# A fused dynamic-convolution and MLP kernel: its fill in another order, with small transposes as warm-up

## The chip, the cores and the metric

One core of a Trainium2 chip runs the whole program. The metric is the device time of one execution in microseconds (us); the time of a kernel is the median of its timed runs. The views of the profile come from one further execution, and durations are taken from that one.

## The reference

Three layers stand behind each other, in fp32. A dynamic convolution weighs the last seven rows of `x` with a softmax over `weight_gen` (2 x 4096 rows of 192, eight heads). A gated layer follows, with 1536 hidden columns, and a layer with `h * cos(h)`, with 2048.

```python
w = exp(weight_gen - max(weight_gen)); w = w / (sum(w) + 1e-9)
x = einsum('bshk,bskhg->bshg', w, x_unf)          # x_unf: seven shifted rows of x
x = (1 / (1 + exp(-(x @ w_gate))) * (x @ w_val)) @ w_out
h = x @ w_in
out = (h * cos(h)) @ w_out2
```

## The kernel before

The 8192 rows are worked on in 16 chunks of 512. A chunk's first layer has 12 steps, its second 8; a step computes two tiles of hidden columns (`hidden`, L413: 18 matmuls of 64 partitions, two row halves side by side), puts them through the nonlinearity, splits the result into a high and a low part (`gh` by ScalarE, `gl` by GpSimd, L556 and L557) and multiplies by the output weights (`out_matmuls`, L432). Every product is made of three: high by high, low by high, high by low.

The program is written in one fixed order (`tc.manual_schedule()`): each engine works off its instructions in the order in which the code issues them, and a wait holds up all that stands behind it on that engine.

The **fill** is what comes before the first full step:

- The softmax weights `sm` of the first two groups (`load_group`, L222; group 0 serves chunk 0, group 1 the next three quarters) and the first input `xp` (`load_x`, L266) are loaded, then the weight units (`Unit.load`, L137: each has a gate part and a value part; `OutUnit.load`, L169). Before the change, `sm` and the value parts of units 0 to 2 go over ScalarE's queue, the rest over SyncE's (SP).
- `softmax_ops` issues on VectorE the maximum (L237), the difference (L240), on ScalarE the exponential (L242), on VectorE sum (L245), reciprocal (L247, L248) and scaling (L251). `s0` and `s1` are the two groups.
- `conv_products(0)` issues the seven products of `xp` with the weights on VectorE (L283: four into `prs`, two into `pr`, one into `acc`). `first_input` transposes each of them on TensorE (`transposes`, L335: 16 matmuls of 64 columns a product, accumulated in the PSUM tiles `po0` and `po2`). Then `split_input` writes the transposed input `xT`: five high pieces each by ScalarE (L357) and VectorE (L359, a cast), then ten low pieces by VectorE (L363).
- A weight unit is decoded by `decode` in two parts: two ScalarE operations (L110, L113), then one of VectorE (L115). Afterwards `split` makes its high part on ScalarE (L120) and its low part on GpSimd (L122). `next(decoding)` issues one piece of that, `run(late)` the splits that have become due. 128x384 is one of the small units 0 and 1, 128x768 a large one or an output unit.
- `steps[:2]` then issue their 24 first matmuls (`mm_high`, L413), and the loop over the steps begins. The first step's product on VectorE is L518.

TensorE has nothing to do until the first product is ready. `warm_up(8)` gives it eight full 128x128 fp32 matmuls on the identity into the four rotating tiles `h`, which nobody reads.

Of the kernel before, what the change touches and what calls it, by code (L numbers as in the profile page):

```python
# [9 lines left out]
F32 = mybir.dt.float32  # L10
# [3 lines left out]
AF = mybir.ActivationFunctionType  # L14
# [15 lines left out]
def dyn_conv_glu_cos_mlp(  # L30
# [11 lines left out]
    nc = tc.nc  # L42
    B, S, D = x.shape
    H, K = weight_gen.shape[2], weight_gen.shape[3]
    G = D // H
    P = 128
# [4 lines left out]
    N = TC * P  # L51
# [6 lines left out]
    HP = P // 2  # L58
# [22 lines left out]
    ps_h = ctx.enter_context(tc.tile_pool(name="ps_h", bufs=4, space=bass.MemoryType.PSUM))  # L81
    ps_o = ctx.enter_context(tc.tile_pool(name="ps_o", bufs=1, space=bass.MemoryType.PSUM))

    ident = const.tile([P, P], F32, name="ident")
    sin_bias = const.tile([P, 1], F32, name="sin_bias")
    warm = const.tile([P, 1], F32, name="warm")
# [128 lines left out]
    def load_group(g, tag, q=nc.sync):  # L215
        t0, t1 = groups[g]
        pool = fpool if tag == "wf" else opool
        s = pool.tile([P, (t1 - t0) * H, K], F32, name="sm", tag=tag)
        cuts = sorted({t0, t1, min(max(t0, T - ROT), t1)})
        for a, b in zip(cuts, cuts[1:]):  # L220
            r = (a + ROT) % T
            q.dma_start(  # L222
                out=s[:, (a - t0) * H:(b - t0) * H, :].rearrange("p a k -> p (a k)"),
                in_=wgr[:, r:r + b - a, :].rearrange("p t c -> p (t c)"),
            )
        for t in range(t0, t1):
            sm[t] = (s, t0)
# [62 lines left out]
    def product_tile():  # L290
        return apool.tile([P, TC, D], F32, name="pr", tag="pr", bufs=2)
# [20 lines left out]
    def conv_products(c):  # L312

        big = tpool.tile([P, K - 3, TC, D], F32, name="prs", tag="xA" if c == LEAD else "xB")
        att[c] = [big[:, k] for k in range(K - 3)] + [product_tile(), product_tile(), acc_tile()]
        for k, pr in enumerate(att[c]):
            tap(c, k, pr)
            yield
# [10 lines left out]
    def transposes(p, src, first, end):  # L329

        blocks = [(0, 0)] + [(2, t) for t in range(TC)] + [(0, t) for t in range(1, TC)]
        for q, t in blocks:
            for h in range(2):
                r = slice(h * HP, (h + 1) * HP)
                nc.tensor.matmul(  # L335
                    p[h][0:min(P, D - q * HP), (2 * q + t) * HP:(2 * q + t + 1) * HP],
                    lhsT=src[r, t, q * HP:min(D, q * HP + P)], rhs=ident[r, r], is_transpose=True,
                    start=first and (q, t) == blocks[0], stop=end and (q, t) == blocks[-1],
                )

    WHOLE, HALVES = slice(0, P), (slice(0, HP), slice(HP, P))
# [49 lines left out]
    def first_input():  # L391

        p = [ps_o.tile([P, N], F32, name="pt", tag=f"po{2 * h}") for h in range(2)]
        for k, _ in enumerate(conv_products(0)):
            transposes(p, att[0][k], k == 0, k == K - 1)
            yield
        xt = xT[1, 0] = tpool.tile([P, 2, NQ, N], F32R, name="xT", tag="xA")
        ops = split_input(xt, p, True)
        next(ops)
        yield  # L400
        for _ in ops:
            pass
# [80 lines left out]
    class Step:  # L483
# [5 lines left out]
        ps = None  # L489
# [88 lines left out]

    TAPS = [1, 1, 2, 2, 0, 2, 1, 1, 1, 2, 1], [0, 0, 0, 2, 0, 2, 2, 2, 2, 2, 2]
    APART = 0, 1, 6, 7, 8, 10, 10  # L580
    NWARM = 8
    SOFT, TAPS0, AHEAD = [0,1,2,3,4], [4,5,6,7,8,9,9], 2
    LEAD = 2
    segments = [(1, c) for c in range(LEAD)]
# [44 lines left out]

    def warm_up(n):  # L630
        for _ in range(n):
            ps = ps_h.tile([P, N], F32, name="pw", tag="h")
            nc.tensor.matmul(ps[:, 0:P], lhsT=ident, rhs=ident, start=True, stop=True)

    def run(ops):
        for f in ops:
            f()
        ops.clear()

    with tc.manual_schedule():  # L640
        nc.gpsimd.memset(sin_bias, SIN_BIAS)
        make_identity(nc, ident)
        load_group(0, "va", nc.scalar)
        load_x(0)
        load_group(1, "o", nc.scalar)
        sp, act = nc.sync, nc.scalar
        units1[0].load(sp, 0)
        units1[0].load(act, 1)
        nc.scalar.activation(out=warm, in_=sin_bias, func=AF.Exp)
        units1[1].load(sp, 0)  # L650
        units1[1].load(act, 1)
        units1[2].load(sp, 0)
# [12 lines left out]
        decoding = chain(units1[:2] + [u for _, u in todo])  # L665
# [4 lines left out]
        s0, s1 = softmax_ops(0), softmax_ops(1)  # L670
        for c in range(1, NCH):
# [15 lines left out]
            if c <= LEAD:  # L687
                n, ops = K, conv_products(c)
# [4 lines left out]
            else:  # L693
                n, ops = 2 * K, conv_ops(c)
# [1 line left out]
            add_side(k0, at, [cost(TC * D)] * n, ops)  # L696
        side.sort(key=lambda e: e[1])

        for ops in [s0] * 3 + [s1] * 2 + [s0] * 2 + [s1] * 3:
            next(ops)  # L700
        nc.scalar.activation(out=warm, in_=sin_bias, func=AF.Sigmoid)
        units1[3].load(sp, 1)
        load_x(1)
        units1[4].load(sp, 0)
# [1 line left out]
        outs1[1].load(sp)  # L706
        for _ in s0:
            pass
        warm_up(NWARM)
        for k, _ in enumerate(first_input()):  # L710
            if k in (5, 6):
                next(decoding)
            if k == 5:
                run(late)
            if k == K:
                run(late)
                next(decoding)
                run(late)
# [24 lines left out]
        for k, st in enumerate(steps):  # L743
            layer, c, j = st.layer, st.c, st.j
            ended = None
            if layer == 1:
# [17 lines left out]
                if k in inputs:  # L764
                    c1 = inputs[k]
                    ops = transpose_ops(att[c1], c1)
# [76 lines left out]
```

## Time and profile before

| | us |
|---|---|
| median of 3 timed runs | 1252.81 (1251.09 to 1253.61) |
| profiled execution, its own time | 1251.61 |
| span of the profiled execution | 1249.8 |
| TensorE matmul busy | 1219.4 (98%) |
| VectorE busy | 902.1 (72%) |
| ScalarE busy | 792.8 (63%) |
| GpSimd busy | 713.0 (57%) |

PE is TensorE's matmuls and PEld its weight loads, which lie beside them; DVE is VectorE, ACT ScalarE, POOL GpSimd, and SPq and ACTq are the queues on which SyncE and ScalarE issue transfers. A row of the timeline merges instructions of one line that follow each other: start, time from the first start to the last end, engine, line, operation, count, and in brackets the idle time ahead of it with what ended that. A busy engine is not one that bounds: what matters is who waits for whom in a stretch.

### The profile page before, as it was taken

The numbers are of one execution on the slowest core, as the hardware profiler recorded it, in microseconds if no ns is written. First come the engines' busy times: TensorE is split into PE (matmuls) and PEld (weight loads), VectorE is DVE, ScalarE is ACT, GpSimd is POOL, SyncE is SP. The second block draws the span as 40 slices with busy tenths as digits, with TensorE's granted clock in tenths as the row PEclk, the third lists the DMA queues.
The fourth block names the chain that finished last, engine by engine and source line by source line (L and its number), as shares of the span: only waits on it lengthen the run. The fifth ranks groups of instructions, "written<-read, shape, count | busy, mean of one in ns | idle before, by whom it ended". The sixth has DMA issues, their size and how long they took to land.

```text
span 1249.8 us, 26898 instructions
## 1 busy us (share of the span) xinstructions
PE 1219.4 (98%) x11056; PEld 1058.3 (85%) x11056; DVE 902.1 (72%) x1309; ACT 792.8 (63%) x1326; POOL 713.0 (57%) x531
## 2 busy tenths in 40 slices
PE   6889999999999999999999999999999999999997
PEld 5677988898898888888898888989889899888886
DVE  7967887777877676877667787775877767683585
ACT  6765856648475574857557485664847557484674
POOL 3958645647465474655637465463746546464563
PEclk8999999999999999999999999999999999999999
DMA  9902202121111211111121120112111121020010
GB/s 250 248 20 58 63 14 69 27 70 27 45 32 34 69 26 54 43 45 27 26 82 27 46 52 14 58 27 74 27 45 26 40 58 26 14 52 14 1 27 26
DMA packets 27403, 61.94 MB, mean 50 GB/s; under 512 B 2580, under 2 KB 7698, under 8 KB 27280
## 3 DMA queue, kind: packets, MB, share of 16 engines
q1 hardware_dynamic: 26368, 59.09, 17.5%
q8 instruction: 86, 1.41, 0.5%
q10 hardware_dynamic: 912, 1.13, 0.3%
q14 instruction: 37, 0.30, 0.1%
HBM read 30.33 MB, written 6.29 MB: 29 GB/s over the span
## 4 chain that ended last, share of the span: by engine, by line
PE 84%; DVE 1%; ACT 1%; issue 0%; DVEq 0%; ACTq 0%
PE ph L413 46%; PE po L432 36%; PE pf L469 1%; PE pt L335 1%; DVE wk L546 0%; ACT wk L542 0%; ACT gh L556 0%; DVE wk L529 0%; DVE wk L532 0%; DVE wk L518 0%; ACT va L441 0%; DVE wk L537 0%; DVE gl L557 0%; ACT wk L536 0%; DVE pr L283 0%
## 5 line engine op out<-in xcount | busy, mean ns | idle before, releaser
L557 POOL TENSOR_TENSOR gl<-wk,gh 128x512 fp32r<-128x512 f32 x446 | 607.0, 1367 | 498.5 <-ACT gh L556 381.3
L413 PE MATMUL ph<-xT,unit 64*128 64x512 f32 x5760 | 772.8, 390 | 8.5 <-DVE wk L518 4.6
L413 PEld LDWEIGHTS ph<-xT,unit 64*128 64x128 f32 x5760 | 617.9, 185 | 104.0 <-DVE wk L518 13.6
L432 PE MATMUL po<-gh,outu 64*128 64x512 f32 x2688 | 552.1, 390 | 2.2 <-ACT gh L556 1.8
L432 PE MATMUL po<-gl,outu 64*128 64x512 f32 x1792 | 467.7, 389 | 4.6 <-POOL gl L557 4.6
L556 ACT ACTIVATE gh<-wk 128x512 fp32r<-128x512 f32 (+1 forms) x450 | 283.1, 629 | 249.1 <-DVE wk L518 206.1
L432 PEld LDWEIGHTS po<-gh,outu 64*128 64x128 f32 x2688 | 405.5, 185 | 37.2 <-ACT gh L556 2.7
L432 PEld LDWEIGHTS po<-gl,outu 64*128 64x128 f32 x1792 | 315.7, 185 | 28.8 <-POOL gl L557 6.4
L518 DVE TENSOR_TENSOR wk<-ph,wk 128x512 f32<-128x512 f32 x192 | 131.7, 686 | 146.4 <-ACT wk L515 136.0
L546 DVE SCALAR_TENSOR_TENSOR wk<-ph,wk 128x512 f32<-128x512 f32 (+1 forms) x258 | 168.4, 687 | 42.5 <-ACT wk L542 42.5
L542 ACT ACTIVATE wk<-wk,sin_bias 128x512 f32<-128x512 f32 (+1 forms) x258 | 173.0, 714 | 19.4 <-DVE wk L532 8.8
L515 ACT ACTIVATE wk<-ph 128x512 f32<-128x512 f32 x192 | 113.6, 592 | 57.8 <-PE ph L413 56.9
L529 DVE TENSOR_SCALAR wk<-ph 128x512 f32<-128x512 f32 x129 | 88.0, 682 | 64.1 <-PE ph L413 62.3
L536 ACT ACTIVATE wk<-ph 128x512 int32<-128x512 f32 x129 | 75.5, 585 | 73.6 <-PE ph L413 73.0
L309 DVE TENSOR_TENSOR acc<-acc,pr 128x768 f32<-128x768 f32 x78 | 102.0, 1308 | 0.4
L283 DVE TENSOR_TENSOR pr<-xp,sm 128x768 f32<-128x768 f32 x84 | 96.0, 1144 | 0.0
L532 DVE SCALAR_TENSOR_TENSOR wk<-wk,ph 128x512 f32<-128x512 f32 x129 | 88.1, 683 | 4.4
L537 DVE TENSOR_TENSOR wk<-wk,ph 128x512 f32<-128x512 int32 x129 | 87.3, 677 | 0.0
L442 DVE TENSOR_TENSOR va<-po,va 128x512 f32<-128x512 f32 x32 | 22.0, 688 | 39.1 <-PE po L432 29.1
L363 DVE TENSOR_TENSOR xT<-pt,xT 64x256 fp32r<-64x256 f32 (+1 forms) x76 | 27.2, 413 | 21.5 <-ACT xT L357 21.3
L357 ACT ACTIVATE xT<-pt 64x256 fp32r<-64x256 f32 (+1 forms) x66 | 20.4, 378 | 21.5 <-PE pt L335 21.3
L122 POOL TENSOR_TENSOR unit<-wf,unit 128x768 fp32r<-128x768 f32 (+1 forms) x11 | 22.2, 2022 | 15.8 <-ACT unit L120 15.8
(61 smaller groups left out, 507.8 us busy)
## 6 DMA issues: line engine op xcount, KB each, us to landing
xT<-xT SPq DMA_DIRECT2D x90, 256.0 KB, 3.9
xp<-in_x_dram SPq DMA_DIRECT2D x13, 960.0 KB, 4.8
out_dram<-o SPq DMA_DIRECT2D x16, 384.0 KB, 2.3
rawo<-in_moe_w_out_dram SPq DMA_DIRECT2D x7, 768.0 KB, 15.9
raw<-in_moe_w_in_dram SPq DMA_DIRECT2D x8, 384.0 KB, 15.7
raw<-in_moe_w_gate_dram SPq DMA_DIRECT2D x5, 384.0 KB, 12.8
raw<-in_moe_w_val_dram SPq DMA_DIRECT2D x4, 384.0 KB, 15.3
sm<-in_weight_gen_dram SPq DMA_DIRECT2D x3, 336.0 KB, 5.1
```

Of the source, the lines that this page charges most:

```text
L283: nc.vector.tensor_tensor(out=out.rearrange("p t (h g) -> p t h g", g=G), in0=xp[c][:, k:k + TC, :].rearrange("p t (h g) -> p t h g", g=G) ...
L309: nc.vector.tensor_tensor(out=acc, in0=acc, in1=last, op=ALU.add)
L413: nc.tensor.matmul(ps[i], lhsT=u.t[r, w, (s + i) % NQ, c0:c0 + P], rhs=xt[r, x, s, :], start=n == 0, stop=n == len(terms) - 1,)
L432: nc.tensor.matmul(po[2 * i + a], lhsT=w[r, d0:d0 + P], rhs=g[r], start=first and g is gh and d0 < D, stop=last and g is gl,)
L515: nc.scalar.activation(out=self.w[0], in_=self.ps[0], func=AF.Sigmoid)
L518: nc.vector.tensor_tensor(out=self.w[0], in0=self.ps[1], in1=self.w[0], op=ALU.mult)
L529: nc.vector.tensor_scalar(out=w, in0=u, scalar1=0.25, scalar2=ROUND_MAGIC, op0=ALU.add, op1=ALU.add)
L532: nc.vector.scalar_tensor_tensor(out=w, in0=w, scalar=ROUND_MAGIC, in1=u, op0=ALU.subtract, op1=ALU.subtract)
L542: nc.scalar.activation(out=w, in_=w, func=AF.Sin, scale=-SIN_SCALE, bias=sin_bias)
L546: nc.vector.scalar_tensor_tensor(out=w, in0=self.ps[i][:, r], scalar=TWO_PI, in1=w, op0=ALU.mult, op1=ALU.mult)
L556: nc.scalar.activation(out=gh, in_=w, func=AF.Copy)
L557: eng.tensor_tensor(out=gl, in0=w, in1=gh.bitcast(F32), op=ALU.subtract)
```

## The change

- **Queues.** Both `sm` loads go over SP's queue, around the first input; ScalarE's queue starts with the table load and has the value parts alone.
- **Softmax.** The two differences of group 1 and its exponential move behind the second product; so does the load of the sigmoid table.
- **Decoding.** The decoding of unit 0 on VectorE moves behind the last product, that of unit 1 and the whole of unit 2 behind the high pieces of `xT`.
- **Warm-up.** Instead of eight large matmuls there are rounds of two small transposes (one in each row half): 24 rounds ahead of the first product, 4, 4, 4, 4, 4 and 2 behind the next six, 10 behind the last. They write the tiles `po1` and `po3`, of which there is one buffer each.

```diff
     def first_input():
         p = [ps_o.tile([P, N], F32, name="pt", tag=f"po{2 * h}") for h in range(2)]
+        warm_up(24)
         for k, _ in enumerate(conv_products(0)):
             transposes(p, att[0][k], k == 0, k == K - 1)
+            warm_up(WARM[k])
             yield
...
-    NWARM = 8
+    WARM = 4, 4, 4, 4, 4, 2, 10
...
     def warm_up(n):
         for _ in range(n):
-            ps = ps_h.tile([P, N], F32, name="pw", tag="h")
-            nc.tensor.matmul(ps[:, 0:P], lhsT=ident, rhs=ident, start=True, stop=True)
+            for r in HALVES:
+                ps = ps_o.tile([P, N], F32, name="pw", tag="po1" if r is HALVES[0] else "po3")
+                nc.tensor.matmul(ps[:, 0:HP], lhsT=ident[r, :], rhs=ident[r, r], is_transpose=True, start=True, stop=True)
...
-        load_group(0, "va", nc.scalar)
+        sp, act = nc.sync, nc.scalar
+        load_group(0, "va")
         load_x(0)
-        load_group(1, "o", nc.scalar)
-        sp, act = nc.sync, nc.scalar
+        load_group(1, "o")
+        nc.scalar.activation(out=warm, in_=sin_bias, func=AF.Exp)
         units1[0].load(sp, 0)
         units1[0].load(act, 1)
-        nc.scalar.activation(out=warm, in_=sin_bias, func=AF.Exp)
...
-        for ops in [s0] * 3 + [s1] * 2 + [s0] * 2 + [s1] * 3:
+        for ops in [s0] * 3 + [s1] * 2 + [s0] * 2:
             next(ops)
-        nc.scalar.activation(out=warm, in_=sin_bias, func=AF.Sigmoid)
...
-        warm_up(NWARM)
         for k, _ in enumerate(first_input()):
-            if k in (5, 6):
+            if k == 1:
+                for _ in range(3):
+                    next(s1)
+                nc.scalar.activation(out=warm, in_=sin_bias, func=AF.Sigmoid)
+            if k == K - 1:
                 next(decoding)
-            if k == 5:
                 run(late)
             if k == K:
+                next(decoding)
                 run(late)
                 next(decoding)
                 run(late)
```

On TensorE, at the start of the program, the order before was this (`pw` is a warm-up's tile, `pt` the transposed products):

```order
L633 MATMUL pw<-ident 128x128 x8
L335 MATMUL pt<-ident,prs 128x64 x2
L335 MATMUL pt<-ident,prs 64x64 x8
L335 MATMUL pt<-ident,prs 128x64 x8
L335 MATMUL pt<-ident,prs 64x64 x8
```

Now it is this, with the semaphore that an instruction waits for in brackets (PE_49 counts TensorE's own finished instructions, DVE_49 those of VectorE, Pool_49 those of GpSimd):

```order
L636 MATMUL pw<-ident 128x64 [waits Pool_49]
L636 MATMUL pw<-ident 128x64
L636 MATMUL pw<-ident 128x64 [waits PE_49] x46
L335 MATMUL pt<-ident,prs 128x64 [waits DVE_49]
L335 MATMUL pt<-ident,prs 128x64
L335 MATMUL pt<-ident,prs 64x64 x8
L335 MATMUL pt<-ident,prs 128x64 x6
L636 MATMUL pw<-ident 128x64 [waits PE_49] x8
```

Every warm-up but the first two waits for TensorE's own earlier one, since a half's tile has one buffer: it waits for the warm-up two places ahead of it.

On VectorE, from the last small products to the low pieces of the transposed input, the order before was this (`wf` is a unit being decoded, from `raw`):

```order
L283 TENSOR_TENSOR pr_165<-xp_103,sm_101 128x768
L115 SCALAR_TENSOR_TENSOR wf_269<-wf_269,raw_107 128x384
L283 TENSOR_TENSOR acc_166<-xp_103,sm_101 128x768
L115 SCALAR_TENSOR_TENSOR wf_273<-wf_273,raw_111 128x384
L359 CAST xT_300<-pt_162 128x4x64
L359 CAST xT_300<-pt_162 64x4x64 x4
L115 SCALAR_TENSOR_TENSOR wf_297<-wf_297,raw_114 128x768
L363 TENSOR_TENSOR xT_300<-pt_161,xT_300 128x4x64
```

Now it is this:

```order
L283 TENSOR_TENSOR pr_241<-xp_103,sm_101 128x768
L283 TENSOR_TENSOR acc_242<-xp_103,sm_101 128x768
L115 SCALAR_TENSOR_TENSOR wf_494<-wf_494,raw_108 128x384
L359 CAST xT_504<-pt_142 128x4x64
L359 CAST xT_504<-pt_142 64x4x64 x4
L115 SCALAR_TENSOR_TENSOR wf_498<-wf_498,raw_111 128x384
L115 SCALAR_TENSOR_TENSOR wf_516<-wf_516,raw_114 128x768
L363 TENSOR_TENSOR xT_504<-pt_141,xT_504 128x4x64
```

The last product stands one decoding earlier; the decoding of unit 1 has moved from ahead of the casts to behind them, ahead of the low pieces.

On ScalarE, around its high pieces of `xT` (L357), the order before was this:

```order
L120 ACTIVATE unit_276<-wf_269 128x384
L110 ACTIVATE wf_297<-raw_114 128x768
L113 ACTIVATE raw_114<-raw_114 128x768
L357 ACTIVATE xT_300<-pt_161 128x4x64
L357 ACTIVATE xT_300<-pt_161 64x4x64 x4
L120 ACTIVATE unit_311<-wf_273 128x384
```

Now it is this:

```order
L120 ACTIVATE unit_501<-wf_494 128x384
L357 ACTIVATE xT_504<-pt_141 128x4x64
L357 ACTIVATE xT_504<-pt_141 64x4x64 x4
L110 ACTIVATE wf_516<-raw_114 128x768
L113 ACTIVATE raw_114<-raw_114 128x768
L120 ACTIVATE unit_519<-wf_498 128x384
```

The two operations on unit 2 (`raw_114`) have moved behind the high pieces. Behind this place the engines' orders are the same in both kernels.

## Rows read from the trace of the kernel before

**Rows 1.** Busy time by stretch: us of each engine (instructions), PEclk, DMA share, GB/s.

```profile
24.00:62.00 38.00, 31.84 (x296) 23.91 (x297) 34.27 (x33) 29.77 (x45) 36.18 (x21) 1.00 1.04 248
...
100.00:600.00 500.00, 497.91 (x4542) 435.25 (x4540) 374.04 (x545) 320.05 (x538) 290.55 (x214) 1.00 0.16 44
```

**Rows 2.** Timeline of VectorE, 0 to 26 us.

```profile
6.21 0.39 DVE L237 TENSOR_REDUCE st<-sm 128x32 f32<-128x224 f32 x1 [6.21 <-DMA sm<-in_weight_gen_dram]
...
7.35 0.67 DVE L237 TENSOR_REDUCE st<-sm 128x32 f32<-128x224 f32 x2
...
8.82 0.62 DVE L240 TENSOR_TENSOR sm<-sm,st 128x224 f32<-128x224 f32 x2
...
9.78 3.57 DVE L283 TENSOR_TENSOR prs<-xp,sm 128x768 f32<-128x768 f32 x4
...
15.00 0.55 DVE L115 SCALAR_TENSOR_TENSOR wf<-wf,raw 128x384 uint32<-128x384 uint32 x1
15.47 0.95 DVE L283 TENSOR_TENSOR acc<-xp,sm 128x768 f32<-128x768 f32 x1
16.34 0.55 DVE L115 SCALAR_TENSOR_TENSOR wf<-wf,raw 128x384 uint32<-128x384 uint32 x1
17.24 2.23 DVE L359 CAST xT<-pt 128x256 fp32r<-128x256 f32 x5 [0.34 <-PE pt L335]
19.49 0.96 DVE L115 SCALAR_TENSOR_TENSOR wf<-wf,raw 128x768 uint32<-128x768 uint32 x1
20.37 3.86 DVE L363 TENSOR_TENSOR xT<-pt,xT 128x256 fp32r<-128x256 f32 x10
...
25.44 0.68 DVE L518 TENSOR_TENSOR wk<-ph,wk 128x512 f32<-128x512 f32 x1
```

**Rows 3.** Timeline of TensorE, 0 to 26 us, and its first 16 transposes alone.

```profile
1.40 3.59 PE L633 MATMUL pw<-ident 128*128 128x128 f32 x16 [1.40 <-POOL ident masks.py:199]
10.80 1.11 PE L335 MATMUL pt<-ident,prs 64*128 64x64 f32 x16 [5.81 <-DVE prs L283]
16.48 0.69 PE L335 MATMUL pt<-ident,acc 64*128 64x64 f32 x16 [0.65 <-DVE acc L283]
18.82 5.20 PE L413 MATMUL ph<-xT,unit 64*128 64x512 f32 x27 [0.21 <-ACT xT L357]
```

**Rows 4.** Waits from 24 to 62 us: who for whom, us in total, times, longest.

```profile
ACT gh L556 <- DVE wk L518: 6.3, 7, 1.5
```

**Rows 5.** Transfers: GB/s from 2 to 6 us, and two loads' KB and us to landing.

```profile
2.00:4.00 2.00, 2.00 (x11) 2.00 (x11) 0.00 (x0) 1.49 (x2) 0.00 (x0) 1.00 0.75 260
4.00:6.00 2.00, 0.99 (x6) 0.79 (x5) 0.00 (x0) 0.00 (x0) 0.00 (x0) 1.00 0.99 389
...
xp<-in_x_dram SPq DMA_DIRECT2D x1, 960.0 KB, 5.2
...
sm<-in_weight_gen_dram ACTq DMA_DIRECT2D x1, 224.0 KB, 6.0
```

**Rows 6.** Transposes by tile: ns of one, min/median/max, first and last start.

```profile
L335 PE MATMUL pt<-ident,prs x64: 311/312/367, 10.8 to 14.2; 64*128 64x64 f32 x32, 64*64 64x64 f32 x32
L335 PE MATMUL pt<-ident,acc x16: 216/220/273, 16.5 to 16.9; 64*128 64x64 f32 x8, 64*64 64x64 f32 x8
```

**Rows 7.** Busy time and PEclk (third number from the end) in stretches of 2 us.

```profile
10.00:12.00 2.00, 1.20 (x22) 1.21 (x24) 2.00 (x3) 1.98 (x5) 0.00 (x0) 0.50 1.07 220
...
14.00:16.00 2.00, 1.83 (x42) 1.64 (x38) 2.00 (x4) 0.41 (x1) 0.00 (x0) 0.78 1.10 274
...
18.00:20.00 2.00, 1.77 (x7) 1.15 (x9) 1.88 (x5) 1.92 (x5) 0.00 (x0) 0.58 1.06 288
```

**Rows 8.** Timeline of ScalarE, 16 to 26 us.

```profile
16.02 0.90 ACT L110 ACTIVATE wf<-raw 128x768 f32<-128x768 f32 x1
...
17.61 1.95 ACT L357 ACTIVATE xT<-pt 128x256 fp32r<-128x256 f32 x5
```

## The prediction

> **What bounds the kernel now.** I read the busy times by stretch first. From 100 to 600 us TensorE's matmuls are busy 497.9 of 500 us [rows 1], and nothing of the change lies there: whatever is won or lost ahead of it goes into the time one for one. From 24 to 62 us it is busy 31.8 of 38 us, while GpSimd is busy 36.2 and VectorE 34.3 [rows 1]. There the decoding of the weights goes along with the steps. The waits of that stretch are of engines for engines, the longest sum of them ScalarE's for the product L518 [rows 4]; no row of them names a weight transfer, though the transfers run without a pause (DMA share 1.04) [rows 1]. So this stretch, too, starts when its first work is ready.
>
> Then the fill, on VectorE's timeline. It waits until 6.21 us for the softmax weights, and from there works nearly without a gap: softmax, seven products, casts, low pieces, until the last low piece at 20.37 + 3.86 = 24.23 us, and the first step's product L518 at 25.44 us [rows 2]. TensorE follows it: the last product's transposes end at 16.48 + 0.69 = 17.17 us [rows 3], the casts start 0.07 us later [rows 2]. I call that end of the transposes E; L518 comes 8.27 us behind it. TensorE's 24 first matmuls lie beside the casts and low pieces: it is done with them and the first low ones by 18.82 + 5.20 = 24.02 us [rows 3], just when VectorE is. L518 is the point that I carry the sum to.
>
> **The change, part by part.**
>
> *Queues.* VectorE now meets group 0 earlier, but its next two instructions read group 1, which stands on SP's queue behind the first input. What must land for them is 112 + 960 + 224 KB, 1.33 MB. By 6.0 us the trace had moved 2 x 260 + 2 x 389 KB, 1.30 MB, and a little ahead of 2 us [rows 5], so I put group 1 at 6.0 us; it is 5.2 us if the better rate held from 2 us on, 7.35 us (where those instructions stand now) if ScalarE's value parts slow it. From there to the first product's start was 9.78 - 7.35 = 2.43 us; without the two differences (0.62 us) it is 1.81 us, and the product is ready 0.95 us later [rows 2]: 8.8 us against 10.73. The value parts start some 0.6 us later, behind the table load; that is hidden, for the decoding that needs them on VectorE (L115) stood at 15.00 us [rows 2], and it too moves behind `acc`. The table loads move to places where ScalarE waits for VectorE: nothing.
>
> *VectorE's order.* The differences only change places (0.62 us earlier out, later in). One decoding of 128x384 leaves the path ahead of `acc`: 15.47 - 15.00 = 0.47 us won [rows 2]. The other moves from under the transposes to behind the casts, 0.47 us lost. Unit 2's ScalarE part (16.02 to 17.61 us, 1.6 us [rows 8]) moves behind the high pieces: ScalarE writes these from E + 0.07, for 1.95 us [rows 8], and needs 1.7 us more for L110 and L113, so VectorE's L115 on unit 2 can start at E + 3.75. Before it started at 19.49, E + 2.32 [rows 2]. That is 1.4 us lost, and it includes the 0.47 us. L518 goes from E + 8.3 to E + 9.7.
>
> *Warm-up.* Here lies the price. Each warm-up waits for the one two places ahead to be finished, so the two of a round run side by side, and the next round waits for them. The trace has no such wait of TensorE for itself. Below, a round costs no more than two transposes in a stream: 0.11 us at 1.2 GHz ((1.11 - 0.31) / 7 for the eight pairs of the first product [rows 3, 6]) and 0.06 us at 2.4 GHz ((0.69 - 0.22) / 7 [rows 3, 6]). Above, it costs one whole matmul behind a wait, 0.367 and 0.273 us (the longest of their groups, which are the first behind a wait [rows 6]), and the 0.06 us from VectorE's end to TensorE's start (15.47 + 0.95 to 16.48 [rows 2, 3]): 0.43 and 0.33 us. I take the upper value: the semaphore counts finished matmuls, and a finished one is what that row measures.
>
> The Trainium skill ("TensorE: Matmul & The Clock Gate", Single matmul latency) gives (219 + N)/1.2 ns and (398 + N)/2.4 ns for one bf16 matmul, 0.24 and 0.19 us at 64 columns. The rows here are longer, 0.37 and 0.27 us, and decide; by the page's figures the end would be an estimated 4 us earlier than by mine.
>
> The clock: it was granted at half (1.2 GHz) when the transposes began at 10.8 us, and at full from about 14.9 us (0.78 on average over 14 to 16 us), with nothing on TensorE in between but transposes; after the pause behind 17.17 us it fell to half again [rows 3, 7]. So I let the 24 rounds, with TensorE mostly waiting, run at half, and let the clock rise 4.1 us behind the first real transposes.
>
> Then: 24 rounds from 1.40 us [rows 3] are 23 waits of 0.43 and one issue, to 11.4 us; the first product is there at 8.8, so TensorE is late from the start. A product with four rounds takes 8 x 0.11 + 3 x 0.43 + 0.11 = 2.28 us at half, 8 x 0.06 + 3 x 0.33 + 0.06 = 1.53 us at full (the first round behind transposes finds its tile free). VectorE makes one each 0.89 us (3.57 / 4 [rows 2]), so TensorE sets the pace. 4.1 us at half are 1.8 products, to 15.5; the other 3.2 take 4.9 us, to 20.4. The sixth, with two rounds, takes 0.87 us, the last 0.69: E = 22.0 us, 4.8 us later than 17.17. With the 1.4 us behind E, L518 comes at 31.7 instead of 25.44 us: **6.2 us later**.
>
> TensorE's ten last rounds end 9 x 0.33 = 3.0 us behind E, and the 24 first matmuls take 4.6 us at the pace of before (5.20 / 27 x 24 [rows 3]): E + 7.6, under the low pieces, which end at E + 8.5. They cost nothing here, by a margin of 0.9 us.
>
> The profiled execution took 1251.61 us, the median is 1252.81, 1.2 us more and inside the runs' own spread. I add the 6.2 us to the median: **1259.0 us** (1257.8 against the profiled execution). Its own range goes from rounds and transposes all at 2.4 GHz (24 rounds to 9.05, five products 7.65, 0.87 and 0.69: E = 18.3; 1.1 + 1.4 = 2.5 us) to the second case below: 1255.3 to 1262.4.
>
> **The rivals.**
>
> *Half clock to the end of the fill.* If TensorE's many short waits keep it at 1.2 GHz, the five products take 11.4 us, the sixth 8 x 0.11 + 0.43 + 0.11 = 1.42, the last 1.11: E = 25.3. Ten rounds (3.9 us) and 24 matmuls (12 pairs of 512 columns at 1.2 GHz, 5.1 us) then end at E + 9.0, past the low pieces, and six more matmuls come before L518: 35.0 us, 9.6 us later, **1262.4 us**. For it: TensorE would do real work little over half of the time. Against it: the transposes alone raised the clock [rows 7].
>
> The Trainium skill ("TensorE: Matmul & The Clock Gate", PE-mode transpose) says that work in transpose mode doesn't bring the full clock. By that rule this rival would hold; this trace disagrees, with PEclk going from 0.50 to full during transposes alone.
>
> *The rounds cost only their issue; not slower.* If a warm-up doesn't hold TensorE for the whole length of the one ahead (the lower bound), 24 rounds end at 1.4 + 2.6 = 4.0 us, long before the first product, and four rounds and a product are 12 x 0.06 = 0.72 us, inside VectorE's 0.89. Then VectorE sets E: group 1 at 6.0, `acc` (which ended 6.64 us behind the first product's start [rows 2]) at 6.0 + 1.81 + 6.64 - 0.47 + 0.62 = 14.6, E = 15.4 to 15.6, and L518 at 25.1 to 25.3: **1252.6 us**, no change; the 1.6 us won ahead of E are given back behind it. With group 1 at 5.2 us it is 1251.7. It decides at a round of about 0.1 us. Beyond 0.2% faster it would have to land at about 3.8 us, and the bytes speak against that.
>
> *The delay is absorbed.* If transfers bound the stretch from 24 to 62 us, a late start would only use up lead: under 2.5 us are left, **1254 us**. For it: the DMA share of 1.04 [rows 1]. Against it: no wait there names a transfer [rows 4].
>
> **How the numbers follow.** Forecast 0.48, half clock 0.16, rounds at issue cost 0.28 (0.06 of it faster by over 0.2%), absorbed 0.08. 0.2% is 2.5 us, about what a measurement of this kernel can tell from no change. Slower by more than that: 0.48 + 0.16 + 0.01 of the absorbed, 0.65; faster 0.06; the same 0.29. The range reaches from the third case with an early landing, 1251.5, to the second with a run's scatter of 1.1 us, 1263.5. The likeliest case's own range stands above.
>
> **What would show it.** Right: the warm-ups' row is 112 long, and its first 48 end near 11 us instead of 5.0; TensorE no longer waits for the products (5.8 us before) but VectorE and ScalarE for the transposes, by some 6 us at the casts; L115 on unit 2 waits for ScalarE; L518 starts near 31.7 us. A single warm-up's start lies 0.33 to 0.43 us behind the one two places ahead. Wrong: starts 0.1 us apart, or the first 48 done by 5 us, or E ahead of 17.2 us. PEclk in 12 to 25 us tells the first rival from the forecast. If L518 is late and the total is not, the fourth case holds, and rows of waits for transfers between 24 and 62 us should be gone or shorter.

## The result and the profile after

| | before | after |
|---|---|---|
| median, us | 1251.99 (1251.09 to 1253.61, 4 runs) | 1263.65 (1261.31 to 1263.98, 4 runs) |
| ratio after/before, 95% interval | | 1.0088, 1.0076 to 1.0100 |
| profiled execution, its span | 1251.61, 1249.8 | 1261.31, 1259.5 |

The changed kernel is slower, by 9.5 to 12.5 us (0.76% to 1.0% of 1252). The prediction had the sign, but too small a size: +6.2 us, where the medians show about +11. Its first rival (half clock to the end of the fill, +9.6) is what the profile shows. The median lies past the likeliest case's own range (1255.3 to 1262.4) and 0.15 us past the upper end of the whole range, 1263.5.

TensorE's timeline of the kernel after, 0 to 37 us (start us, us, engine, line, tile; in brackets the idle time ahead and what ended it). L636 is a warm-up, L335 the transposes, L415 the step's first matmuls (L413 before):

```profile
1.40 10.14 PE L636 MATMUL pw<-ident 64*128 64x64 f32 x48 [1.40 <-POOL ident masks.py:199]
11.85 1.12 PE L335 MATMUL pt<-ident,prs 64*128 64x64 f32 x16 [0.32 <-DVE prs L283]
12.76 1.62 PE L636 MATMUL pw<-ident 64*128 64x64 f32 x8
14.14 1.09 PE L335 MATMUL pt<-ident,prs 64*128 64x64 f32 x16
...
23.07 1.09 PE L335 MATMUL pt<-ident,pr 64*128 64x64 f32 x16
23.93 0.77 PE L636 MATMUL pw<-ident 64*128 64x64 f32 x4
24.46 1.09 PE L335 MATMUL pt<-ident,acc 64*128 64x64 f32 x16
25.31 4.16 PE L636 MATMUL pw<-ident 64*128 64x64 f32 x20
29.20 6.21 PE L415 MATMUL ph<-xT,unit 64*128 64x512 f32 x37
```

Against [rows 3]: the first warm-ups end at 11.54 us instead of 4.99; a product with its four rounds takes 14.14 - 11.85 = 2.29 us, later ones 2.23; E, the end of the last transposes, is 24.46 + 1.09 = 25.55 us against 17.17. Two tables by tile (ns of one, min/median/max; first and last start) say why. The first is that of the warm-ups' `pw`; its last row is TensorE's wait for itself, in us and times:

```profile
L636 PE MATMUL pw<-ident x112: 311/366/367, 1.4 to 29.1; 64*128 64x64 f32 x112
...
  PE pw L636: 10.2, 48
```

The second is that of the real transposes' `pt`:

```profile
L335 PE MATMUL pt<-ident,prs x64: 311/311/367, 11.9 to 19.4; 64*128 64x64 f32 x32, 64*64 64x64 f32 x32
...
L335 PE MATMUL pt<-ident,pr x32: 311/311/313, 20.8 to 23.9; 64*128 64x64 f32 x16, 64*64 64x64 f32 x16
...
L335 PE MATMUL pt<-ident,acc x16: 311/311/312, 24.5 to 25.2; 64*128 64x64 f32 x8, 64*64 64x64 f32 x8
```

In [rows 6] the last product's transposes took 220 ns, those of 2.4 GHz; now all seven products are at the 311 ns of 1.2 GHz. (PEclk is of no use here: the trace has no clock record before 32 us, and the page then prints full. The durations tell it.)

VectorE's timeline of the kernel after:

```profile
2.86 0.39 DVE L237 TENSOR_REDUCE st<-sm 128x32 f32<-128x224 f32 x1 [2.86 <-DMA sm<-in_weight_gen_dram]
...
8.80 0.68 DVE L237 TENSOR_REDUCE st<-sm 128x32 f32<-128x224 f32 x2 [5.14 <-DMA sm<-in_weight_gen_dram]
...
16.67 0.94 DVE L283 TENSOR_TENSOR acc<-xp,sm 128x768 f32<-128x768 f32 x1
17.53 0.55 DVE L115 SCALAR_TENSOR_TENSOR wf<-wf,raw 128x384 uint32<-128x384 uint32 x1
25.59 2.23 DVE L359 CAST xT<-pt 128x256 fp32r<-128x256 f32 x5 [7.51 <-PE pt L335]
27.85 0.56 DVE L115 SCALAR_TENSOR_TENSOR wf<-wf,raw 128x384 uint32<-128x384 uint32 x1
29.27 0.96 DVE L115 SCALAR_TENSOR_TENSOR wf<-wf,raw 128x768 uint32<-128x768 uint32 x1 [0.87 <-ACT raw L113]
30.15 3.87 DVE L363 TENSOR_TENSOR xT<-pt,xT 128x256 fp32r<-128x256 f32 x10
...
35.22 0.68 DVE L520 TENSOR_TENSOR wk<-ph,wk 128x512 f32<-128x512 f32 x1
```

Three things differ from [rows 2]. Group 0 lands early (2.86 us), but group 1 at 8.80 us is late. VectorE has the last product ready at 17.6 us and then waits 7.51 us for TensorE. Behind the casts stands the new wait for ScalarE, 0.87 us. The first product of the steps, L520 (L518 before), starts at 35.22 us, 9.78 us later than before.

From there nothing is absorbed: the last one of the 192 starts at 1177.87 us after and 1168.11 before, 9.76 us apart. So all of the profiled execution's loss (9.7 us in both its time and its span) arises ahead of 35.22 us.

### The profile page after: what moved, and what is told of

Read it like the earlier page. It is cut to its first block, busy times and chain, and to the rows that moved or that the text cites. A ratio compares the mean times of both kernels' runs of the same rounds, so it can differ in the third digit from the quotient of the medians.

```text
span 1259.5 us, 27088 instructions
## 1 busy us (share of the span) xinstructions
PE 1235.2 (98%) x11152; PEld 1055.7 (84%) x11152; DVE 901.8 (72%) x1309; ACT 793.2 (63%) x1326; POOL 712.7 (57%) x531
## 4 chain that ended last, share of the span: by engine, by line
PE 83%; DVE 1%; ACT 1%; issue 0%; DVEq 0%; ACTq 0%
PE ph L415 46%; PE po L434 35%; PE pf L471 1%; PE pt L335 1%; DVE wk L548 0%; ACT wk L544 0%; ACT gh L558 0%; DVE wk L520 0%; DVE wk L531 0%; DVE wk L534 0%; DVE acc L309 0%; ACT va L443 0%; ACT wk L517 0%; DVE wk L539 0%; DVE gl L559 0%
## 5 line engine op out<-in xcount | busy, mean ns | idle before, releaser
L415 PE MATMUL ph<-xT,unit 64*128 64x512 f32 x5760 | 772.7, 389 | 7.2 <-DVE wk L520 4.6
L415 PEld LDWEIGHTS ph<-xT,unit 64*128 64x128 f32 x5760 | 613.0, 185 | 107.7 <-DVE wk L520 13.5
L434 PE MATMUL po<-gh,outu 64*128 64x512 f32 x2688 | 551.9, 389 | 2.2 <-ACT gh L558 1.8
L434 PE MATMUL po<-gl,outu 64*128 64x512 f32 x1792 | 467.6, 388 | 4.6 <-POOL gl L559 4.6
L434 PEld LDWEIGHTS po<-gh,outu 64*128 64x128 f32 x2688 | 404.5, 184 | 40.0 <-ACT gh L558 2.7
L434 PEld LDWEIGHTS po<-gl,outu 64*128 64x128 f32 x1792 | 315.6, 184 | 30.5 <-POOL gl L559 6.2
L520 DVE TENSOR_TENSOR wk<-ph,wk 128x512 f32<-128x512 f32 x192 | 131.7, 686 | 146.5 <-ACT wk L517 129.5
L357 ACT ACTIVATE xT<-pt 64x256 fp32r<-64x256 f32 (+1 forms) x66 | 20.4, 378 | 28.4 <-PE pt L335 28.2
```

Of the source, the lines that this page charges most:

```text
L415: nc.tensor.matmul(ps[i], lhsT=u.t[r, w, (s + i) % NQ, c0:c0 + P], rhs=xt[r, x, s, :], start=n == 0, stop=n == len(terms) - 1,)
L434: nc.tensor.matmul(po[2 * i + a], lhsT=w[r, d0:d0 + P], rhs=g[r], start=first and g is gh and d0 < D, stop=last and g is gl,)
L520: nc.vector.tensor_tensor(out=self.w[0], in0=self.ps[1], in1=self.w[0], op=ALU.mult)
```

## The experiments

All times are medians; the ratio is against the runs of the kernel before in the same group (1251.94, 1252.65, 1251.60 and 1251.26 us). The ratio and its 95% interval in brackets are taken over the runs, so a ratio need not be the quotient of two medians.

**Warm-ups taken out of the changed kernel.** The queues and the order of VectorE stay.

```diff
-        warm_up(24)
...
             transposes(p, att[0][k], k == 0, k == K - 1)
-            warm_up(WARM[k])
```

> The changed kernel without any warm-up. If the waiting rounds are the loss (theory), TensorE follows VectorE again: group 1 of the softmax weights still lands at 8.8 us, the last product ends at 17.6, its transposes at 18.3 to 18.7, the first step's product (L520) starts at 28.0 to 28.4 us instead of 35.2, and the time is 2.5 to 3 us above the kernel before. If the slow clock is the loss whatever the waits (rival), the time stays over 6 us above it. If the late softmax weights are the main loss (second rival), it stays over 6 us above it as well, and L520 past 31 us.

Measured: 1255.43 us, ratio 1.0029 (1.0019 to 1.0040), L518 at 28.90 us. TensorE's timeline:

```profile
12.65 1.97 PE L335 MATMUL pt<-ident,prs 64*128 64x64 f32 x32 [12.65 <-DVE prs L283]
14.89 1.72 PE L335 MATMUL pt<-ident,prs 64*128 64x64 f32 x32 [0.28 <-DVE prs L283]
16.63 0.69 PE L335 MATMUL pt<-ident,pr 64*128 64x64 f32 x16
...
18.37 0.69 PE L335 MATMUL pt<-ident,acc 64*128 64x64 f32 x16 [0.18 <-DVE acc L283]
```

E falls from 25.55 to 19.06 us (18.3 to 18.7 was expected; group 1 was read at 9.51 us in this execution, at 8.80 in the changed kernel's). The first two products take 1.97 us, the fifth and the last 0.69 each (216 ns a transpose): with nothing but transposes on TensorE the clock rises by 16.6 us. The warm-ups cost about (1.0088 - 1.0029) x 1252 = 7.4 us (4.5 to 10.1 by the ends of the intervals); 3.6 us (2.4 to 5.0) of the loss come from the rest of the change.

**Warm-ups that don't wait.** The same 112, in eight column slots of one tile a half, so that no round waits for the one ahead.

```diff
-                ps = ps_o.tile([P, N], F32, name="pw", tag="po1" if r is HALVES[0] else "po3")
-                nc.tensor.matmul(ps[:, 0:HP], lhsT=ident[r, :], ...)
+                nc.tensor.matmul(ps[:, c:c + HP], lhsT=ident[r, :], ...)
```

> The changed kernel with the same 112 warm-up transposes, but written into eight column slots of one tile a half, so that none waits for an earlier one. Theory: the first 48 end at about 4.0 us instead of 11.5, a product with four rounds takes 0.7 us (2.4 GHz) to 1.3 us (1.2 GHz) instead of 2.24, the last transposes end at 18.3 to 20.6, L520 starts at 28 to 30.3 us and the time is 2.5 to 5 us above the kernel before. Rival (transposes as such keep the clock low, and that is the loss): transposes at 311 ns to the end, and over 6 us above. If the clock follows how tightly TensorE's work stands, the transposes fall to 216 ns before the last product.

Measured: 1256.07 us, ratio 1.0039 (1.0026 to 1.0051), L520 at 28.82 us. TensorE's timeline (L641 is the warm-up):

```profile
1.41 2.82 PE L641 MATMUL pw<-ident 64*128 64x64 f32 x48 [1.41 <-POOL ident masks.py:199]
11.92 1.12 PE L335 MATMUL pt<-ident,prs 64*128 64x64 f32 x16 [7.70 <-DVE prs L283]
12.83 0.63 PE L641 MATMUL pw<-ident 64*128 64x64 f32 x8
13.26 1.06 PE L335 MATMUL pt<-ident,prs 64*128 64x64 f32 x16
...
17.10 0.68 PE L335 MATMUL pt<-ident,pr 64*128 64x64 f32 x16
```

The 48 end at 4.2 us instead of 11.5, a product with four rounds takes 1.28 to 1.34 us at 1.2 GHz instead of 2.23, and from 17.10 us the transposes are at full clock. E is 19.10. So it is the waits, and the clock that comes with them, that cost: 6.4 us at L520, (1.0088 - 1.0039) x 1252 = 6 us in time (3.1 to 9.3 by the ends of the intervals). How that divides between waits and clock no run separates. Without waits the 112 are cheap, and win nothing: L520 stands 0.08 us from where it stands with none at all, and here group 1 was read 0.63 us earlier (8.88 against 9.51 us).

**Only the new warm-ups,** in the kernel before.

```diff
+        warm_up(24)
...
             transposes(p, att[0][k], k == 0, k == K - 1)
+            warm_up(WARM[k])
...
-    NWARM = 8
+    WARM = 4, 4, 4, 4, 4, 2, 10
...
-        warm_up(NWARM)
```

The body of `warm_up` is that of the change.

> The kernel before with nothing but the new warm-ups. Theory: the first 48 end at 11.5 us, five products at 2.24 us, one at 1.4, the last 1.1: the last transposes end at 25.1 us, and with ten waiting rounds and 24 matmuls at 1.2 GHz TensorE itself is late for the first step's product: 33.4 to 35 us instead of 25.4, the time 8 to 10 us above the kernel before. Rival (the late softmax weights are the loss): under 3 us above.

Measured: 1262.26 us, ratio 1.0083 (1.0069 to 1.0097), L520 at 34.56 us, E at 24.95 us. Of its transposes by tile, those of the last product:

```profile
L335 PE MATMUL pt<-ident,acc x16: 311/311/313, 23.8 to 24.6; 64*128 64x64 f32 x8, 64*64 64x64 f32 x8
```

and on its VectorE timeline the first product of the steps:

```profile
34.56 0.69 DVE L520 TENSOR_TENSOR wk<-ph,wk 128x512 f32<-128x512 f32 x1 [1.28 <-ACT wk L517]
```

The warm-ups alone make 9.1 of the 9.8 us, and again every transpose is at 311 ns. Taken out of the change they give back only 28.90 - 35.22, 6.3 us. The two needn't agree, since the other parts of the change are partly covered while the warm-ups are there: a late group 1 by TensorE's first 24 rounds, which last to 11.5 us anyway, and the moved decoding by the time in which L520 would have waited 1.28 us for the first matmuls and ScalarE. The rows bear this out: E is 0.60 us later in the changed kernel (25.55 against 24.95), and L520 follows E after 9.67 us instead of 9.61, together the 0.66 us between 34.56 and 35.22.

**Only the new queues,** in the kernel before.

```diff
-        load_group(0, "va", nc.scalar)
+        load_group(0, "va")
         load_x(0)
-        load_group(1, "o", nc.scalar)
+        load_group(1, "o")
+        nc.scalar.activation(out=warm, in_=sin_bias, func=AF.Exp)
```

> The kernel before with nothing but the new queues (both softmax loads around the first input on SyncE's queue, ScalarE's queue with the value parts alone, table load first). Theory: the value parts, issued from 0.9 us, share the transfers with the first input, group 1 lands at 8.8 us, VectorE starts its chain there instead of at 7.35, and the time is 1.0 to 1.5 us above the kernel before. The prediction on record (group 1 at 6.0 us) would give 1.3 us below it.

Measured: 1253.33 us, ratio 1.0012 (1.0003 to 1.0021), L518 at 27.61 us, 2.17 later. Timeline of all engines and queues:

```profile
0.74 1.28 ACT L647 ACT_TABLE_LOAD   x1 [0.74 <-PEq L827]
...
0.88 1.38 ACTq L137 DMA_DIRECT2D raw<-in_moe_w_val_dram  x2
...
7.99 1.14 POOL L268 COPY xp<-xp 128x1152 f32<-128x1152 f32 x1 [6.64 <-DMA xp<-in_x_dram]
...
9.51 0.68 DVE L237 TENSOR_REDUCE st<-sm 128x32 f32<-128x224 f32 x2 [5.83 <-DMA sm<-in_weight_gen_dram]
```

This edit loses 2.17 us at L518 and 1.5 us in time (0.4 to 2.6), where I had it win 1.35 (group 1 at 6.0 instead of 7.35). ScalarE's queue issues the value parts at 0.88 us, inside the table load (0.74 to 2.02). Before they stood behind both `sm` loads and started at 1.67 us. That the table load doesn't hold the queue could be read from the kernel before, whose second value part is issued inside it:

```profile
2.40 1.28 ACT L649 ACT_TABLE_LOAD   x1 [2.40 <-issue]
2.46 1.33 ACTq L137 DMA_DIRECT2D raw<-in_moe_w_val_dram  x2
```

Now 768 KB of weights run beside the input: GpSimd's copy of the input starts at 7.99 us (6.04 before) and group 1 is read at 9.51 us instead of 7.35 [rows 2].

**Only the new places of the decoding,** in the kernel before.

```diff
-            if k in (5, 6):
+            if k == K - 1:
                 next(decoding)
-            if k == 5:
                 run(late)
             if k == K:
+                next(decoding)
```

> The kernel before with nothing but the new places of the decodings. Theory: the last product ends 0.47 us earlier, but behind the transposes VectorE has one more small decoding and waits for ScalarE's part of unit 2: the low pieces start 1.4 us later relative to the end of the transposes, L518 at 26.4 instead of 25.4 us, the time 1.0 us above the kernel before. Rival (the casts ahead of the decoding win TensorE time that VectorE does not give back): no later than before.

Measured: 1252.54 us, ratio 1.0009 (1.0000 to 1.0018), L518 at 26.49 us, 1.05 later. In time the edit alone isn't clear of noise (0 to 2.3 us by the interval, and the medians are 1252.54 and 1252.65); the place of L518 is the witness here. On VectorE's timeline the wait that was worked out stands alone:

```profile
20.54 0.96 DVE L115 SCALAR_TENSOR_TENSOR wf<-wf,raw 128x768 uint32<-128x768 uint32 x1 [1.01 <-ACT raw L113]
```

**No rounds between the products.** In the changed kernel, the 24 ahead and the 10 behind kept.

```diff
-    WARM = 4, 4, 4, 4, 4, 2, 10
+    WARM = 0, 0, 0, 0, 0, 0, 10
```

> The changed kernel with the 24 waiting rounds ahead of the first product and the ten behind the last, and none between the products. Theory: the 24 end at 11.5 us, just as the first product is there, and the ten lie under the casts and low pieces, so all of the warm-ups' price lies in the 22 rounds between products: L520 at 28.5 to 29.5 us instead of 35.2, the time 3 to 5 us above the kernel before, as without any warm-up. Rival (the rounds ahead and behind cost as well): L520 past 31 us, over 6 us above.

Measured: 1256.21 us, ratio 1.0036 (1.0024 to 1.0048), L520 at 28.68 us, E at 18.88 us. TensorE's timeline:

```profile
1.40 10.17 PE L636 MATMUL pw<-ident 64*128 64x64 f32 x48 [1.40 <-POOL ident masks.py:199]
12.31 1.99 PE L335 MATMUL pt<-ident,prs 64*128 64x64 f32 x32 [0.75 <-DVE prs L283]
...
18.17 0.71 PE L335 MATMUL pt<-ident,acc 64*128 64x64 f32 x16
```

The 24 rounds ahead of the first product and the 10 behind the last cost nothing: the time is that without any warm-up (1255.43, the intervals overlap). All of the warm-ups' price is the 22 rounds between the products. Counted from the read of group 1, which differs between the executions (8.80, 9.51, 8.88 and 9.27 us), the first step's product comes 26.42 us behind it in the changed kernel, 19.39 without warm-ups, 19.94 with warm-ups that don't wait, and 19.41 here: the 22 waiting rounds cost 7.0 us, the 112 warm-ups that don't wait 0.55. With waits in front alone the clock rises, too: the last product's 16 transposes take 0.71 us.

**Value parts behind the first exponential.** If the value parts delay the input, holding them back should win. The kernel before, with the softmax loads and the input on SP's queue, and ScalarE's loads issued after the first exponential.

```diff
+        load_group(0, "va")
+        load_x(0)
+        load_group(1, "o")
...
+        for _ in range(3):
+            next(s0)
+        for i in range(3):
+            units1[i].load(act, 1)
```

> The kernel before with the new queues for softmax weights and first input, but the value parts of units 0 to 2 issued behind the first exponential on ScalarE instead of ahead of it. Theory (the value parts, issued at 0.9 us on the other queue, took the transfers' rate from the first input): the first input lands near 5.2 and group 1 near 6.0 us instead of 8 and 9.5, the first product starts at 8.4 instead of 9.8, L518 near 24.1, the time 1.3 us below the kernel before. Rival (one queue alone is slow): group 1 lands past 7.4 us again and nothing is won.

Measured: 1252.41 us, ratio 1.0001 (0.9992 to 1.0010). The input is copied at 6.10 us and group 1 read at 7.10 us (VectorE was free for it from 3.7 us); the first L518 is at 25.21 us, 0.23 earlier. Then the weights are late, on ScalarE's timeline:

```profile
27.40 0.91 ACT L110 ACTIVATE wf<-raw 128x768 f32<-128x768 f32 x1 [0.83 <-DMA raw<-in_moe_w_val_dram]
```

and the second L518 starts at 29.60 us, against 28.89 before. The early landing did not come; but without the value parts beside it group 1 lands as before again, so the delay with the new queues was theirs.

**The input first, group 1's softmax behind the second product** (on top of the last one; warm-ups and decoding as before).

```diff
-        for ops in [s1] * 2 + [s0] * 2 + [s1] * 3:
+        for ops in [s0] * 2:
             next(ops)
-        nc.scalar.activation(out=warm, in_=sin_bias, func=AF.Sigmoid)
...
         for k, _ in enumerate(first_input()):
+            if k == 1:
+                for _ in range(5):
+                    next(s1)
+                nc.scalar.activation(out=warm, in_=sin_bias, func=AF.Sigmoid)
```

> As the run before, and VectorE's first two operations on group 1 stand behind the second product too, so that nothing ahead of the products needs group 1. Theory: the first product starts when the first input has landed, at 5.4 us instead of 9.8; 1.3 us of group 1's softmax come in between; L518 at 22.3 instead of 25.4 us, the time 3 us below the kernel before, decodings permitting. Rival (the weights become the bound): ScalarE waits for unit 0 to 3 to land, and less than 1 us is won.

Measured: 1252.63 us, ratio 1.0003 (0.9994 to 1.0012). The first product starts at 5.94 us (9.78 before), the first L518 at 24.32. E is only 1.3 us earlier (15.89 us): VectorE does group 1's softmax between the second product and the third, and all transposes are at 311 ns. On TensorE's timeline:

```profile
7.90 1.99 PE L335 MATMUL pt<-ident,prs 64*128 64x64 f32 x32 [2.72 <-DVE prs L283]
10.83 1.99 PE L335 MATMUL pt<-ident,prs 64*128 64x64 f32 x32 [0.94 <-DVE prs L283]
```

The idle time ahead of the first transposes is shorter than before (2.72 against 5.81 us [rows 3]), and a second one, of 0.94 us, lies ahead of the third product's. Why the clock didn't rise here isn't shown. On ScalarE's timeline:

```profile
27.16 0.90 ACT L110 ACTIVATE wf<-raw 128x768 f32<-128x768 f32 x1 [1.49 <-DMA raw<-in_moe_w_val_dram]
```

The second L518 starts at 29.37 us, 0.48 later than before: the head start of 1.12 us became a wait for weights.

**The same, all parts on one queue in the order of need** (gate and value part of a unit behind each other).

```diff
         for i in range(3):
             units1[i].load(sp, 0)
+            units1[i].load(sp, 1)
+        outs1[0].load(sp)
+        units1[3].load(sp, 0)
...
-        for i in range(3):
-            units1[i].load(act, 1)
-        outs1[0].load(sp)
-        units1[3].load(sp, 0)
```

> The kernel before with the softmax weights, the input and all of the first weight parts on SP's queue in the order in which they are needed (gate and value part of a unit behind each other), the second group's softmax behind the second product. The runs with the value parts issued late (first product at 5.94 us, first L518 at 24.32) lost the head start to weights: second L518 at 29.37 us against 28.89 before. Theory A (the order of the parts was at fault, the value parts of units 0 to 2 stood behind too much): with the parts in order ScalarE's L110 waits for a transfer by under 0.5 us in sum up to 30 us, the second L518 starts at 28.0 us or earlier, and the median is about 1 us below that of before, 1251.5. Theory B (from 2 us on the transfers run without a pause at 200 to 390 GB/s, so the bytes and not their order decide): the waits on transfers stay over 1.5 us in sum, the second L518 starts at 28.9 us or later, and the median is that of before within 0.2%. Theory of the first rival (the clock): the transposes lie at 311 ns in either case, since TensorE pauses ahead of the first product.

Measured: 1251.64 us, ratio 0.9999 (0.9990 to 1.0008). The order was at fault for the weights: the waits on transfers fall to 0.5 and 0.2 us and the second L518 starts at 28.12 us (under 0.5 in sum and 28.0 were expected). The clock went otherwise than expected: the first product's 16 transposes take 0.69 us, those of 2.4 GHz, and only then the transposes go to 311 ns, so the pause ahead of the first product (2.70 us here) doesn't bring the half clock by itself. VectorE's timeline shows where the lead goes. The eleventh L518 and the twelfth:

```profile
60.33 0.69 DVE L518 TENSOR_TENSOR wk<-ph,wk 128x512 f32<-128x512 f32 x1 [1.18 <-ACT wk L515]
...
70.40 0.69 DVE L518 TENSOR_TENSOR wk<-ph,wk 128x512 f32<-128x512 f32 x1
```

Before they stand at 61.50 and 70.04 us. In this execution a lead of 1.17 us is turned into a lag of 0.36. Between them lie the transposes of the second input. Busy times by stretch of 2 us in this run (third number from the end: PEclk):

```profile
60.00:62.00 2.00, 2.00 (x43) 2.00 (x40) 0.69 (x1) 0.30 (x1) 2.00 (x2) 0.50 1.07 343
62.00:64.00 2.00, 2.00 (x54) 2.00 (x52) 0.00 (x0) 0.00 (x0) 0.69 (x1) 0.68 1.09 412
```

In the kernel before, the same stretches:

```profile
60.00:62.00 2.00, 1.63 (x55) 1.63 (x57) 0.82 (x2) 1.14 (x3) 2.00 (x2) 1.00 0.66 129
62.00:64.00 2.00, 2.00 (x67) 2.00 (x63) 0.26 (x2) 0.12 (x1) 1.87 (x2) 1.00 0.91 373
```

Here the clock was granted at half while 62 transposes of the second input ran (3.05 us against 2.04). The weights went nearly as the first theory has it, the median as the second; neither had named the place where the lead is lost. Such a stretch on the second input also shows in the profiles without warm-ups (0.50 in 64 to 66 us), with those that don't wait (0.50 in 66 to 68), with the new warm-ups alone (0.50 in 70 to 72) and with the decoding alone (0.50 in 62 to 64), and in neither profile of the changed kernel. From the eleventh L518 to the twelfth it is 10.06 to 10.07 us in the profiles that have it and 8.54 to 8.55 in the others. Spans of single executions differ by these 1.5 us, so the first places of L518 and the medians are the better witnesses. That the other runs on one queue lose their lead here isn't shown; only one was profiled.

**The changed kernel once more.** Its profiled execution (1261.31 us) lies 2.3 us under its other runs.

> The changed kernel once more, for a second profiled execution. Open is why its other timed runs (1263.6 to 1264.0 us) lie 2.3 us above the profiled one (1261.31), when the fill explains 9.8 us. Theory A (a stretch at 1.2 GHz behind the fill that some executions have and others not: the profile of the new warm-ups alone shows one at 68 to 74 us, that of the changed kernel none there, and the one-queue run one at 60 to 64 us in which 62 transposes took 3.05 us against 2.04): an execution with a time of 1263 us or more shows PEclk at 0.50 somewhere between 60 and 80 us, one of 1261.3 doesn't; L520 starts at 35.0 to 35.4 us in both. Theory B (the fill itself scatters, through the landing of the second group): the first L520 starts at 37 us or later in an execution of 1263 us or more, and PEclk shows no further drop. The median over the runs is 1263.5 +- 0.5 us by both.

Measured: 1263.01 us (1261.27 to 1264.00, 4 runs), ratio 1.0090 (1.0073 to 1.0107); the profiled execution took 1262.61 us. Neither theory was met: at 1262.61 us this execution lies between the times that they speak of, and it shows neither a half-clock stretch in 60 to 80 us nor a late fill. L520 starts at 35.41 us, 0.19 later, and the last of the 192 at 1178.16, 0.29 later; PEclk is 1.00 from 56 to 78 us. The span is 1260.8 us, 1.3 longer than the first profile's, and the other 1.0 us is lost in the program's last products (L434). TensorE's timeline of this run:

```profile
1251.41 1.22 PE L434 MATMUL po<-gh,outu 64*128 64x512 f32 x4 [1.15 <-ACT gh L558]
...
1253.29 0.63 PE L434 MATMUL po<-gl,outu 64*128 64x512 f32 x2
```

and of the first profile of the changed kernel:

```profile
1251.05 0.73 PE L434 MATMUL po<-gh,outu 64*128 64x512 f32 x4 [1.13 <-ACT gh L558]
...
1252.09 0.39 PE L434 MATMUL po<-gl,outu 64*128 64x512 f32 x2
```

Matmul pairs of 0.63 us against 0.39, at a PEclk of 0.50 in 1252 to 1254 us against 1.00. So one execution of the same program differs from another in when the clock falls in the tail. That this, or a stretch as in the run on one queue, explains the runs at 1263.4 to 1264.0 as well isn't shown: those weren't profiled.

## Why the prediction was right, and where it was too small

It was right on the sign and on a round's price, but the case that came was its first rival (0.16), not its likeliest (0.48). By its own steps:

- **What bounds.** Right. The delay at the first step's product passes through the whole program (9.78 us at the first, 9.76 at the last of 192). The fourth case, a delay absorbed from 24 to 62 us, is out. So is its third case: rounds at issue cost would have ended the first 48 at 4.0 us.
- **A round's price.** Right: 0.43 us was forecast at half clock, and the rounds start 0.42 us apart (24 end at 11.54 us, 11.4 forecast). The upper bound, one whole matmul (366 ns here) and the hand-over, was the right one. A product with four rounds at half clock: 2.28 forecast, 2.23 measured.
- **The clock: the step that failed.** I let it rise 4.1 us behind the first real transposes, as before, "with nothing on TensorE in between but transposes". With waiting rounds between the products it never rose in the fill. The five products took 2.29 + 4 x 2.23 = 11.2 us, where the forecast had 1.8 at half and 3.2 at full clock, 9.0; the sixth 1.39 instead of 0.87, the last 1.09 instead of 0.69; and the first began at 11.85 instead of 11.4 (0.14 us by the rounds, 0.31 as its data came late). That is 2.2 + 0.5 + 0.4 + 0.45 = 3.55 us, all of the gap between E = 22.0 and 25.55. It is the first rival's sum (E = 25.3, L518 at 35.0) within 0.3 us. Transposes alone raised the clock before [rows 6, 7], without warm-ups, and behind 24 waiting rounds; with rounds that don't wait between them it rose as well; with waiting rounds between them it didn't, in any of the three profiles that have them. But with the input first all transposes lay at 311 ns, from 7.90 to 15.89 us, with no rounds between them: "nothing in between but transposes" is no sure sign of a rise either. What it is about the waiting rounds no run separates.
- **The rule on transposes.** The Trainium skill ("TensorE: Matmul & The Clock Gate", PE-mode transpose) says that transpose mode doesn't bring the full clock. Its outcome occurred, its reason did not: the run without warm-ups has transposes alone on TensorE, and they go from 311 to 216 ns.
- **Queues: wrong in sign, hidden in the result.** I put group 1 at 6.0 us and the bounds at 5.2 and 7.35, the upper one for a load slowed by the value parts; it was read at 8.80 to 9.51. The step that failed is "The value parts start some 0.6 us later, behind the table load". The queue doesn't wait for the table load, which the trace of before showed already (2.46 us, above); they start 0.8 us earlier than before and take their share of the DMA engines while the input is on its way. In the changed kernel this is nearly covered by the rounds; the edit alone costs 2.17 us at L518 and 1.5 us in time. Without the value parts beside it group 1 was read at 7.10 us, still not at 6.0; why isn't shown.
- **VectorE's order.** Right. 1.4 us behind E were forecast (9.7 from E to the first product), and it is 35.22 - 25.55 = 9.67. As an edit by itself it costs 1.05 us at L518: 1.58 behind E, less 0.53 by which E comes earlier (16.64 us).
- **The last ten rounds.** Right for this kernel: at half clock they end at 25.31 + 4.16 = 29.47 us, 3.9 us behind E as in the first rival, and L520 still shows no wait for TensorE. The margin is gone, though: with the warm-ups alone, where VectorE is earlier, L520 waits 1.28 us.
- **The size against the median.** The two medians of the changed kernel lie 11.7 us above before; its profiled executions 9.7 and 11.0. Of the difference, 9.8 is the fill's. The rest is, in the one execution where it was seen, a half-clock stretch in the tail; for the medians it isn't shown.

## What to carry to other kernels

Dummy matmuls that rotate through one buffer wait for each other, and between pieces of real work each round is paid at a whole latency (0.42 us here); in front of the work, where the engine is idle, the same rounds were free. Whether a warm-up raised the clock is read from the durations of the real matmuls behind it, 311 or 216 ns here, not from how busy the engine looks. And a load that is first on its queue isn't first on the DMA engines if another queue can start its own at the same moment: look at when each queue issues.

## What was not expected of the hardware

- TensorE's clock stayed at 1.2 GHz from 1.4 to 25.2 us although matmuls lay on it most of that time (48 warm-ups over 10.14 us, then a product with its rounds each 2.23 us); between the rounds it waited some 0.2 us each time, 10.2 us in 48 waits.
- ScalarE's table load (0.74 to 2.02 us) doesn't hold up the transfers that its queue issues: they go out at 0.88 us.
- The same program has half-clock stretches at different places in different executions: in the two profiles of the changed kernel the clock falls inside 1250 to 1252 us (0.84) in one and behind 1254 us (0.52) in the other, which is worth 1.0 us.
